# A new table of planner settings for a fused attention and MLP-mixer kernel

## Chip, cores, metric

The kernel runs on one core of a Trainium2 chip. The metric is the device time of one launch in microseconds (us); the figure of a kernel is the median of several runs.

## What is computed

Two blocks read the same input x (2048 tokens of 512) and are mixed by a gate per token: 32-head attention with a head size of 16, and a token-shifting MLP of four weight matrices with two layer norms and two GELUs. Everything is bf16 in memory.

```python
def _A_ref(x, wqkv, wo):
    qkv = (x @ wqkv).reshape(B, S, 3, H, Dh)      # S=2048, H=32, Dh=16
    scores = jnp.einsum("bhqd,bhkd->bhqk", q, k) * (Dh ** -0.5)
    p = softmax(scores, axis=-1)
    o = jnp.einsum("bhqk,bhkd->bhqd", p, v)
    return o.reshape(B, S, D) @ wo

def _B_ref(x, w1, w2, w3, w4):
    h = gelu(layernorm(x) @ w1)
    # the four quarters of h's channels are shifted by 1, -1, 2 and -2 tokens
    hs = shifted(h) @ w2
    x1 = x + hs
    return x1 + gelu(layernorm(x1) @ w3) @ w4     # w3: 512 x 1792

g = sigmoid((x * gate_w).sum(-1, keepdims=True))
out = g * _A_ref(x, ...) + (1 - g) * _B_ref(x, ...)
```

## The kernel before

**Tiles.** A score tile is 128 keys by 512 queries of one head: 32 heads, 16 key blocks and 4 query blocks make 2048 of them. A *round* is a query block, a group of eight heads and one of its two halves, so four heads and 64 tiles; there are 32 rounds. TensorE makes a score tile with one matmul on 32 of its rows (L1320) into one of eight PSUM banks. The exponential is then taken in one of two ways.

- *On ScalarE (ACT):* `issue_act` takes two tiles in two banks and one ACTIVATE turns both into bf16 probabilities (L1415, 128x1024). One matmul per tile then multiplies them into the round's accumulator bank (L1544). The planner costs it with `hold = 0.833 * 512 * w + 51.5` ns for w tiles.
- *On VectorE (DVE):* `issue_dve` takes one tile, and one TENSOR_SCALAR writes 16-bit integers whose bits, read as bf16, are an approximate power of two (L1446, 128x512; called p1 below). Two such tiles are a *pair*. `close_pair` gives the pair three more copies with a constant added to the bits, each one instruction on 128x1024, here called a *shift*; the four copies are summed by the accumulating matmuls, four per tile where an ACT tile has one. A shift runs on DVE or on GpSimd (POOL); both are at L1489/L1491.

`close_pair` (L1466) decides the engine of the three shifts of each pair. It adds `GP2` to a counter and, when that passes one, the pair is *both*: one shift on DVE, two on POOL. It adds `1 - GP3` to a second counter and, when that passes one, the pair is *alone*: all three on DVE. A pair that starts when no more than `URG` tiles (`URG_L` in the last round) of its round are left is alone too, and alone wins over both. Any other pair has two shifts on DVE and one on POOL.

**The other work.** The projections, the MLP matmuls (L953, L964) and their evacuations on DVE, the GELUs on ACT (L1187, L1224) and the layer norms are woven into the same stream with due positions.

**The order.** Everything is issued in an order that is worked out when the kernel is built: `Sim` is a small event model with a fixed duration for every operation. `run` steps through it; whenever TensorE is free, `pe_pick` (L1718) chooses what goes next, and `try_engine` (L330) takes the job of lowest priority number that is ready for each other engine. The chosen start times sort the emission (L1915), so each engine's instruction stream is fixed. The chip only adds semaphore waits: a matmul waits until the last reader of its bank is done, an ACTIVATE waits for its matmuls, and a POOL operation waits for the last DVE operation placed ahead of it in `in_port_order` (L315), which keeps a single order among the operations that share a port of SBUF.

`pe_pick` is steered by some forty settings in `K`. They start from `BASE` (L505), and every eight score tiles (`SEG = 8`, 256 segments) the entry of `STEPS` (L530) for that segment, where there is one, overwrites some of them. Those the prediction speaks of, besides the three above:

- `LIMD` (L1401): new matmul groups other than ACT's start only while fewer than so many banks are held by something else than ACT's tiles and the accumulators.
- `ACC2` (L1514): how many rounds ahead a second accumulator bank may be opened.
- `CAP3`, `CAP2` (L1731): an ACT group of three (two) tiles is taken if ACT then holds no more than so many banks. `CAP3` is 0 in all of the kernel before, so all its groups have two tiles but one.
- `DVE_STOP` (L1373): no DVE tile is taken from a round with so few tiles left; `AHEAD` (L1371): a tile of the next round may be taken once so few are left in this one.

Of the kernel before, what the change touches and what calls it, by code (L numbers as in the profile page):

```python
# [189 lines left out]
class Sim:  # L190
    SWITCH = {"row": 104.0, "col": 104.0, "full": 96.0}
    ISSUE = 4.0
    EARLY = {"ACT": 100.0, "DVE": 75.0}
# [259 lines left out]
def kernel(  # L453
# [52 lines left out]
        P1_PRIO=0.414,  # L506
        S_PRIO=0.38,
        GP2=0.0,
# [19 lines left out]
    )  # L528
    SEG = 8
    STEPS = {  # L530
        0: dict(GP2=0.8, DVE_STOP=13, DVE_ALONE=-158, SL0=60, PRESS=43, DUE_SH=0),
        1: dict(SL0=130, PRESS=26, MAXU=4, ROT=0),
        2: dict(ROT=3),
        3: dict(GP3=0.9, PRESS=15, ROT=1),
        5: dict(S_PRIO=0.625, GP3=0.967, DVE_STOP_L=12, SL0=60, IDLE_NS=700, DVE_WAIT=4, AHEAD2=16, PRESS=26, MAXU=9,
            ROT=2, DUE_SH=-14, AT_SH=34),
        6: dict(AGE=20000, JOIN=1),
        7: dict(PV_IDLE=0.117, MAXU=5, LIMD=4),
        8: dict(GP2=1),
        9: dict(P1_PRIO=0.743),  # L540
        10: dict(E_PRIO=0.25),
        11: dict(ROT=3),
        12: dict(AHEAD=16),
        13: dict(DVE_WAIT=2),
        14: dict(DVE_WAIT=4, AHEAD=9),
        15: dict(B_LOW=8),
        16: dict(URG_L=18, SL0=0),
        17: dict(DVE_STOP=6, URG=8),
        18: dict(AGE=6000),
        20: dict(S_PRIO=0.178, ROT=0),  # L550
        22: dict(DVE_STOP=4, JOIN=0),
        23: dict(LIMD=3),
        24: dict(GP3=1),
        27: dict(E_PRIO=0.1),
        30: dict(E_PRIO=2),
        32: dict(GP3=0.9, SL1=0, AT_SH=118),
        33: dict(DVE_ALONE=2, BRES=2, PV_FULL=0.97),
        34: dict(S_PRIO=0.214, GP2=0),
        35: dict(S_PRIO=0.178, GP2=1, DVE_ALONE=-158, BRES=0, PV_FULL=0.916),
        36: dict(AT_SH=0),  # L560
        38: dict(B_LOW=3, AT_SH=118),
        39: dict(P1_PRIO=0.414, AHEAD2=13, MAXU=3),
        41: dict(DVE_STOP=6),
        42: dict(P1_PRIO=0.279, DVE_STOP=4),
        44: dict(E_PRIO=0.1),
        45: dict(GP3=0.967),
        46: dict(AGE=20000),
        48: dict(E_PRIO=0.4),
        49: dict(DVE_STOP=6, E_PRIO=0.1, AGE=12000),
        50: dict(MAXG=2),  # L570
        51: dict(E_PRIO=0.4),
        52: dict(E_PRIO=2),
        53: dict(AGE=20000),
        54: dict(B_LOW=0, AT_SH=69),
        55: dict(AT_SH=96),
        56: dict(B_LOW=3, AT_SH=118, AGE=12000),
        59: dict(MAXU=4, AFIRST=2),
        61: dict(P1_PRIO=0.312),
        69: dict(MAXG=1),
        70: dict(AHEAD2=24, ROWM=7),  # L580
        71: dict(DUE_SH=-9, AGE=20000),
        72: dict(URG=11, ROWM=5),
        73: dict(DVE_STOP=8),
        74: dict(GP2=0.8, DVE_STOP=4, URG=8, ROWM=7),
        78: dict(AHEAD=3),
        79: dict(PRESS=18),
        86: dict(SL1=60),
        87: dict(URG=5, SL1=0),
        89: dict(GP3=0.9),
        90: dict(B_LOW=2, PV_FULL=0.97),  # L590
        92: dict(ROT=1),
        93: dict(CAP2=5),
        94: dict(SL0=-75, DVE_WAIT=2, HOLE=2),
        95: dict(B_LOW=8, DVE_WAIT=3, DUE_SH=-6),
        96: dict(PV_FULL=0.86),
        97: dict(GP2=0.5, DVE_STOP=6),
        98: dict(DVE_ALONE=500),
        99: dict(URG=11),
        100: dict(DVE_STOP=4, ROWM=99),
        101: dict(JOIN=1),  # L600
        102: dict(IDLE_NS=537, ROT=2, AFIRST=0, AGE=3000, ROWM=7, JOIN=0),
        104: dict(P1_PRIO=0.279),
        105: dict(DVE_ALONE=2),
        106: dict(DVE_ALONE=-158, AHEAD=9),
        107: dict(URG=5),
        108: dict(DVE_ALONE=500, BRES=4, HOLE=3),
        109: dict(URG=3, DVE_ALONE=138),
        111: dict(URG_L=12, IDLE_NS=864),
        112: dict(GP2=0.315),
        113: dict(DVE_ALONE=362),  # L610
        114: dict(ROT=3),
        115: dict(ROT=2),
        116: dict(DUE_SH=16, AGE=12000),
        117: dict(DUE_SH=-6, AGE=3000),
        118: dict(ROT=1),
        119: dict(GP3=0.967, EARLY=64, AGE=20000),
        120: dict(DVE_ALONE=138),
        121: dict(URG=2, PV_FULL=0.947),
        122: dict(GP2=0.15, BRES=0),
        123: dict(DVE_ALONE=-158),  # L620
        124: dict(DVE_STOP=6, SL0=0, JOIN=1),
        126: dict(IDLE_NS=700, HOLE=7),
        127: dict(P1_PRIO=0.55, PV_FULL=0.86),
        128: dict(GP3=1),
        130: dict(PV_FULL=0.97),
        131: dict(EARLY=99, ROWM=3),
        133: dict(URG=8),
        135: dict(P1_PRIO=0.136, GP3=0.967, DVE_STOP_L=14, PRESS=15),
        136: dict(MAXU=9),
        137: dict(GP2=0),  # L630
        138: dict(DVE_STOP=4),
        139: dict(AT_SH=96, JOIN=0),
        140: dict(DVE_ALONE=-81, PV_IDLE=0.731),
        141: dict(GP3=0.633, AHEAD=5, PV_FULL=0.813),
        143: dict(URG=5, MAXU=7),
        145: dict(MAXU=4, ROT=2),
        146: dict(PV_IDLE=0.117),
        147: dict(PV_IDLE=0.731, MAXU=7, ROT=1),
        148: dict(GP2=0.5),
        151: dict(MAXG=2, AGE=12000),  # L640
        152: dict(MAXG=1, AGE=20000),
        153: dict(DUE_SH=-14),
        154: dict(URG=8, AHEAD2=16, HOLE=3),
        155: dict(URG=5, AHEAD2=24, DUE_SH=-6, HOLE=7, MAXG=2, AGE=12000),
        156: dict(S_PRIO=0.38, IDLE_NS=459),
        157: dict(S_PRIO=0.178, DVE_ALONE=138, IDLE_NS=700, DUE_SH=-14, MAXG=1, AGE=3000),
        159: dict(DVE_WAIT=2),
        160: dict(HOLE=3),
        161: dict(DVE_STOP=6),
        162: dict(E_PRIO=0.25),  # L650
        163: dict(AHEAD=12, CAP2=6, LIMA=4),
        167: dict(B_LOW=3, PRESS=26),
        171: dict(S_PRIO=0.3, GP2=1, GP3=0.967, DVE_STOP=13, DVE_STOP_L=16, URG=3, DVE_ALONE=-158, SL0=60, SL1=60,
            IDLE_NS=864, B_LOW=5, DVE_WAIT=3, AHEAD=24, PV_IDLE=0.117, PRESS=18, MAXU=4, AT_SH=69, HOLE=2, MAXG=2,
            E_PRIO=2, AFIRST=2, AGE=6000, ROWM=7, LIMA=3),
        172: dict(DVE_STOP=6),
        173: dict(B_LOW=2),
        174: dict(E_PRIO=0.25),
        175: dict(MAXU=7, HOLE=7),
        176: dict(MAXG=1),  # L660
        177: dict(AT_SH=34),
        178: dict(AT_SH=0),
        179: dict(AT_SH=34),
        180: dict(B_LOW=3, ROWM=5),
        181: dict(ROT=0, GATE=3, ACC2=1),
        184: dict(URG=11),
        185: dict(SL0=0),
        186: dict(S_PRIO=0.178),
        187: dict(IDLE_NS=459),
        188: dict(PV_IDLE=0.5),  # L670
        189: dict(DVE_ALONE=-81),
        190: dict(JOIN=1),
        191: dict(ACC2=0),
        192: dict(S_PRIO=0.214, PV_FULL=0.86, ROWM=3, ACC2=1),
        193: dict(AHEAD=7, PV_FULL=0.947),
        194: dict(PV_FULL=0.97, ROWM=5),
        195: dict(URG=8),
        196: dict(AT_SH=118),
        198: dict(ROT=2),
        199: dict(HOLE=0),  # L680
        200: dict(ROWM=7),
        201: dict(B_LOW=8, AFIRST=0, JOIN=0),
        202: dict(MAXU=3),
        203: dict(MAXU=7),
        204: dict(P1_PRIO=0.743, S_PRIO=0.3, GP2=0, GP3=1, DVE_STOP=4, DVE_STOP_L=7, URG=2, DVE_ALONE=2, EARLY=64,
            SL0=60, SL1=0, IDLE_NS=537, B_LOW=5, DVE_WAIT=2, AHEAD=24, PV_FULL=0.813, PV_IDLE=0.117, MAXU=4, ROT=3,
            DUE_SH=-9, HOLE=7, MAXG=2, CAP2=5, AGE=3000, LIMA=4, JOIN=1),
        205: dict(SL1=60),
        206: dict(DVE_STOP_L=12, SL1=0, MAXU=2, ROT=2, DUE_SH=-14, LIMD=4, ACC2=0, JOIN=0),
        207: dict(SL1=60, AGE=12000),  # L690
        208: dict(SL1=130),
        209: dict(URG=3, ROT=3, ROWM=5),
        210: dict(URG=2, ROT=2, ROWM=7),
        211: dict(DVE_WAIT=4, PV_FULL=0.916, ROT=1, AT_SH=96),
        213: dict(S_PRIO=0.38, HOLE=3),
        214: dict(S_PRIO=0.3, DVE_STOP_L=7, SL0=130, SL1=0, DVE_WAIT=2, PV_FULL=0.813, ROT=2, AT_SH=118, HOLE=7, LIMD=3,
            AGE=3000, JOIN=1),
        215: dict(GP2=0.15),
        216: dict(SL1=-75, PV_IDLE=0.731),
        217: dict(URG=8, B_LOW=8, MAXG=1),  # L700
        220: dict(DVE_STOP=6),
        222: dict(HOLE=3, AGE=20000),
        225: dict(HOLE=7, AGE=3000),
        226: dict(DVE_WAIT=3),
        227: dict(GP2=0.655, CAP2=6),
        228: dict(HOLE=3, GATE=2),
        229: dict(JOIN=0),
        230: dict(GP2=0.15, AT_SH=34, HOLE=7, CAP2=5, GATE=3, ROWM=3, JOIN=1),
        231: dict(B_LOW=3),
        233: dict(PRESS=8),  # L710
        234: dict(GP3=0.9),
        237: dict(DVE_ALONE=138),
        238: dict(PRESS=11),
        239: dict(SL0=-75, MAXU=9, CAP2=4),
        240: dict(URG_L=18, PRESS=18, CAP2=6),
        242: dict(DVE_STOP=13, URG=11, HOLE=2),
        243: dict(MAXU=3),
        246: dict(DVE_STOP=6, URG=8, MAXU=9, HOLE=7),
        248: dict(S_PRIO=0.625, GP2=0.5, PV_FULL=0.86),
        251: dict(PRESS=57),  # L720
        252: dict(SL0=0, LIMA=2),
    }
    K = SimpleNamespace(**BASE)

# [1249 lines left out]
```

## Time and profile before

| what | value |
|---|---|
| median of 3 runs | 754.83 us (753.9 to 755.6) |
| profiled execution, its own time | 750.92 us |
| its span, first to last instruction | 749.1 us |
| ACT busy | 733.0 us (98%), 771 instructions |
| DVE busy | 689.9 us (92%), 1450 instructions |
| POOL busy | 423.3 us (57%), 422 instructions |
| PE busy | 735.9 us (98%), 9516 matmuls |
| DMA | 46 GB/s mean, 17.40 MB read, 6.81 MB written |

Each figure is the union of an engine's instruction spans. Matmul ends are modelled, so PE's 98% doesn't say that TensorE has no room. ACT's and DVE's spans of successive instructions overlap by some 0.1 to 0.2 us, so the pace of a series is read from their start times, not from the mean duration.

The span is cut below into eight stretches of 256 score tiles each, by the start of every 256th matmul of L1320 (at 8.44, 104.17, 199.5, 289.4, 384.94, 470.69, 557.0 and 654.14 us). "DVE busy" is of the stretch; p1 and shifts are counts of instructions that start in it.

| eighth | p1 | shifts on DVE | shifts on POOL | DVE busy us of us |
|---|---|---|---|---|
| 0 | 48 | 24 | 41 | 87.11 of 95.73 |
| 1 | 73 | 51 | 61 | 90.08 of 95.33 |
| 2 | 60 | 45 | 44 | 87.67 of 89.90 |
| 3 | 82 | 74 | 50 | 91.10 of 95.54 |
| 4 | 70 | 77 | 27 | 81.27 of 85.75 |
| 5 | 68 | 50 | 51 | 78.07 of 86.31 |
| 6 | 78 | 70 | 50 | 88.89 of 97.14 |
| 7 | 70 | 74 | 36 | 83.45 of 94.96 |

### The profile page before, as it was taken

To read this page: it belongs to the slowest core of one execution; us is meant where nothing else is said; L and a number is where in the kernel's file an instruction comes from. 1 tells how busy PE (TensorE), PEld (TensorE's weight loads), DVE (VectorE), ACT (ScalarE), POOL (GpSimd) and SP (SyncE) were. 2 spreads that over 40 slices of the span, in tenths; PEclk is the share of its full clock that TensorE was granted. 3 is DMA by queue.
4 is the path that set the end of the run, shared out by engine and by line. 5 is a ranking of instruction groups with operands and counts; after the bars stand their busy time and mean duration, and the time that the engine had idled before them with its cause. 6 is when DMAs were issued, how large, how long until landed. Compare 5 with 4: busy or idle time off the path is not lost.

```text
span 749.1 us, 23684 instructions
## 1 busy us (share of the span) xinstructions
PE 735.9 (98%) x9516; PEld 211.6 (28%) x9516; DVE 689.9 (92%) x1450; ACT 733.0 (98%) x771; POOL 423.3 (57%) x422
## 2 busy tenths in 40 slices
PE   8999999999999999999999999999999999999997
PEld 5343222232222222222322222222222232222222
DVE  5899999998999999999899999998999889989987
ACT  7999999999999999999999999999999999999996
POOL 2355667687674665566555432646767645553552
PEclk9999999999999999999999999999999999999999
DMA  9413322012122211034000110011100000101001
GB/s 197 146 34 85 83 62 49 19 47 79 54 65 68 63 28 49 20 81 109 10 25 9 38 36 27 14 28 47 25 20 21 21 12 28 27 25 21 7 21 47
DMA packets 67095, 34.60 MB, mean 46 GB/s; under 512 B 46749, under 2 KB 62381, under 8 KB 66985
## 3 DMA queue, kind: packets, MB, share of 16 engines
q1 hardware_dynamic: 66040, 32.56, 17.4%
q8 instruction: 74, 1.21, 0.7%
q10 hardware_dynamic: 944, 0.52, 0.2%
q14 instruction: 37, 0.29, 0.1%
HBM read 17.40 MB, written 6.81 MB: 32 GB/s over the span
## 4 chain that ended last, share of the span: by engine, by line
PE 86%; ACT 7%; DVE 4%; issue 2%; POOL 0%; DMA 0%; ACTq 0%; DVEq 0%; POOLq 0%
PE banks L1544 30%; PE banks L1320 30%; PE banks L953 25%; ACT prob L1415 6%; DVE prob L1446 1%; DVE prob L1489 1%; PE banks L932 0%; POOL prob L1491 0%; ACT L1415 0%; DVE st L1128 0%; DVE kT L1025 0%; DMA xn_dram<-xn 0%; PE banks L984 0%; DVE hT L1185 0%; DVE xn L1148 0%
## 5 line engine op out<-in xcount | busy, mean ns | idle before, releaser
L1415 ACT ACTIVATE prob<-banks 128x1024 bf16<-128x1024 f32 x750 | 688.7, 1149 | 1.1 <-PE banks L1320 0.6
L1491 POOL TENSOR_SCALAR prob<-prob 128x1024 uint16<-128x1024 uint16 x360 | 370.2, 1045 | 280.5 <-DVE prob L1489 145.5
L1446 DVE TENSOR_SCALAR prob<-banks 128x512 uint16<-128x512 f32 x549 | 364.1, 684 | 30.3 <-PE banks L1320 25.0
L1544 PE MATMUL banks<-prob,V 128*17 128x512 bf16 (+1 forms) x3695 | 321.3, 382 | 1.2 <-POOL prob L1491 0.7
L1320 PE MATMUL banks<-q,kT 32*128 32x512 bf16 x2048 | 282.7, 385 | 6.1 <-ACT prob L1415 3.4
L1489 DVE TENSOR_SCALAR prob<-prob 128x1024 uint16<-128x1024 uint16 (+1 forms) x465 | 181.2, 434 | 5.3 <-PE banks L1544 2.5
L1320 PEld LDWEIGHTS <-kT 32*128 32x128 bf16 x2048 | 71.1, 91 | 316.4 <-ACT prob L1415 291.0
L1544 PEld LDWEIGHTS <-V 128*17 128x17 bf16 (+1 forms) x3695 | 72.0, 88 | 117.3 <-issue 97.8
L953 PE MATMUL banks<-xnT,w 128*32 128x512 bf16 x1152 | 98.0, 383 | 0.0
L953 PE MATMUL banks<-w,hT 128*32 128x512 bf16 x688 | 63.8, 384 | 0.0
L1583 POOL TENSOR_TENSOR oT<-accsb,bcs 128x512 bf16<-128x512 f32 x31 | 39.8, 1282 | 28.5 <-DVE prob L1489 14.4
L953 PEld LDWEIGHTS <-w 128*32 128x32 bf16 x1936 | 42.4, 95 | 47.3 <-issue 27.7
L953 PE MATMUL banks<-w,w 128*32 128x256 bf16 (+1 forms) x784 | 39.1, 308 | 0.1
L953 PE MATMUL banks<-w,hB 128*32 128x512 bf16 x448 | 37.3, 382 | 0.0
L964 PE MATMUL banks<-wo,oD 32*128 32x512 bf16 x76 | 28.8, 385 | 0.0
L1565 DVE COPY accsb<-banks 128x512 f32<-128x512 f32 x31 | 21.2, 685 | 1.4 <-PE banks L1544 1.0
L1128 DVE BATCH_NORM_STATS2 st<-x_sb 128x6 f32<-128x512 bf16 x32 | 21.8, 685 | 0.0
L953 PE MATMUL banks<-w,wq 128*32 128x512 bf16 x256 | 20.9, 383 | 0.0
L953 PEld LDWEIGHTS <-hT 128*32 128x32 bf16 x688 | 14.8, 95 | 19.1 <-issue 14.9
L953 PE MATMUL banks<-wo,oD 128*32 128x512 bf16 x164 | 20.0, 385 | 0.1
L1217 DVE CAST hB<-banks 128x512 bf16<-128x512 f32 x28 | 19.0, 680 | 1.1 <-PE banks L953 1.1
L1217 DVE CAST hT<-banks 128x512 bf16<-128x512 f32 x28 | 19.0, 680 | 0.4 <-PE banks L953 0.4
(95 smaller groups left out, 262.1 us busy)
## 6 DMA issues: line engine op xcount, KB each, us to landing
bcs<-rr SPq DMA_DIRECT2D x124, 64.0 KB, 2.1
xn_dram<-xn SPq DMA_DIRECT2D x32, 128.0 KB, 1.8
w<-in_B_w_dram SPq DMA_DIRECT2D x5, 512.0 KB, 7.8
oD<-oT SPq DMA_DIRECT2D x124, 16.0 KB, 2.1
w<-in_B_w_dram SPq DMA_DIRECT2D x4, 448.0 KB, 3.2
out_dram<-ot SPq DMA_DIRECT2D x14, 128.0 KB
x_sb<-in_A_x_dram SPq DMA_DIRECT2D x3, 512.0 KB
w<-in_A_wqkv_dram SPq DMA_DIRECT2D x2, 256.0 KB, 5.8
```

The source lines that it names most:

```text
L953: units.append([Op("col", j, lambda j=j, lf=lf, rf=rf, n0=n0, n1=n1, st=st, sp=sp: nc.tensor.matmul(get()[32 * j:32 * j + 32, n0:n1], lhsT ...
L964: o = Op("row", i, lambda: nc.tensor.matmul(get(), lhsT=lf(0, P)[rows], rhs=rf()[rows], start=False, stop=True, tile_position=(32 * i, 0), ...
L1128: a = dve(600, deps, lambda: nc.vector.bn_stats(out=sb.slot[:], in_=x_sb[:, t, :]), prio=6, at=at, acq=[sb])
L1217: pre.append(evac(g, PSUM_NS, lambda ps, m=m: nc.vector.tensor_copy(out=h2()[:, m, :], in_=ps[:])))
L1320: o = Op("row", i, lambda: nc.tensor.matmul(dst(), lhsT=kT[G][32 * i:32 * i + 32, kt * P:(kt + 1) * P], rhs=qbuf[G, c].slot[32 * i:32 * i ...
L1415: job = act(hold, ops, lambda: nc.scalar.activation(out=prob[:, pb.cut(), :].bitcast(BF16), in_=unit()[:, rb.cut(), :], func=ACT.Exp, scal ...
L1446: return nc.vector.tensor_scalar(out=prob[:, b0.cut() if w == 2 else b0.bufs[h0].slot, :], in0=unit()[:, rb.cut() if w == 2 else rb.bufs[0 ...
L1489: return nc.vector.tensor_scalar(out=cut(k), in0=cut(0), scalar1=float(SHIFT * k), scalar2=None, op0=ALU.add)
L1491: return nc.gpsimd.tensor_scalar(out=cut(k), in0=cut(0 if both else 2), scalar1=1.0, scalar2=float(SHIFT * (k if both else 1)), op0=ALU.mu ...
L1544: return nc.tensor.matmul(one(accs[r])[32 * i:32 * i + n, :], lhsT=lhs(n), rhs=rhs(), start=st and not edge, stop=True, tile_position=(0, ...
L1565: e = dve(PSUM_NS, round_ops[r], lambda: nc.vector.tensor_copy(out=ab.slot[:], in_=one(accs[r])), acq=[ab], prio=0, frees=[accs[r], Call(a ...
L1583: n = gp(1250, d3, lambda: nc.gpsimd.tensor_tensor(out=ob.slot[:], in0=ab.slot[:], in1=bb.slot[:], op=ALU.mult), acq=[ob], frees=[ab, bb], ...
```

## The change

The dictionary `STEPS` is replaced as a whole: 185 segments had an entry, 215 have one after. `BASE`, `Sim`, its durations and every function stay as they are, so the same tiles and the same matrices are worked on; what differs is the order of each engine's stream, which score tiles go to DVE instead of ACT, and which engine makes which shift. Nothing is added or removed by hand. The entries for segments 128 to 159, and those elsewhere that set `LIMD` or `CAP3`:

```diff
     STEPS = {
...
-        7: dict(PV_IDLE=0.117, MAXU=5, LIMD=4),
...
-        23: dict(LIMD=3),
...
-        128: dict(GP3=1),
-        130: dict(PV_FULL=0.97),
-        131: dict(EARLY=99, ROWM=3),
-        133: dict(URG=8),
-        135: dict(P1_PRIO=0.136, GP3=0.967, DVE_STOP_L=14, PRESS=15),
-        136: dict(MAXU=9),
-        137: dict(GP2=0),
-        138: dict(DVE_STOP=4),
-        139: dict(AT_SH=96, JOIN=0),
-        140: dict(DVE_ALONE=-81, PV_IDLE=0.731),
-        141: dict(GP3=0.633, AHEAD=5, PV_FULL=0.813),
-        143: dict(URG=5, MAXU=7),
-        145: dict(MAXU=4, ROT=2),
-        146: dict(PV_IDLE=0.117),
-        147: dict(PV_IDLE=0.731, MAXU=7, ROT=1),
-        148: dict(GP2=0.5),
-        151: dict(MAXG=2, AGE=12000),
-        152: dict(MAXG=1, AGE=20000),
-        153: dict(DUE_SH=-14),
-        154: dict(URG=8, AHEAD2=16, HOLE=3),
-        155: dict(URG=5, AHEAD2=24, DUE_SH=-6, HOLE=7, MAXG=2, AGE=12000),
-        156: dict(S_PRIO=0.38, IDLE_NS=459),
-        157: dict(S_PRIO=0.178, DVE_ALONE=138, IDLE_NS=700, DUE_SH=-14, MAXG=1, AGE=3000),
-        159: dict(DVE_WAIT=2),
...
+        61: dict(DVE_STOP_L=7, LIMD=4),
...
+        77: dict(LIMD=4, LIMA=2),
...
+        123: dict(DVE_STOP=6, ROT=2, CAP3=6),
+        124: dict(DVE_STOP=4, ROT=1, CAP3=0),
...
+        129: dict(DVE_STOP=8, IDLE_NS=374, E_PRIO=0.25),
+        130: dict(DVE_STOP=4, IDLE_NS=864, E_PRIO=2),
+        131: dict(GP2=0.655, GP3=1, SL1=0, B_LOW=2, PV_FULL=0.97, PRESS=18, MAXU=4, E_PRIO=0.4),
+        132: dict(DVE_STOP=8, CAP3=6),
+        134: dict(ROT=3),
+        136: dict(ROT=0),
+        137: dict(CAP3=0),
+        138: dict(SL0=-75),
+        140: dict(P1_PRIO=0.312, ROT=3, DUE_SH=32),
+        142: dict(P1_PRIO=0.279, ROT=0, DUE_SH=-6),
+        144: dict(GP3=0.9, MAXU=3),
+        145: dict(CAP2=6),
+        146: dict(URG=11),
+        147: dict(S_PRIO=0.38),
+        148: dict(GP3=0.8),
+        149: dict(GP3=0.9),
+        150: dict(GP3=0.8),
+        151: dict(GP2=0.8),
+        152: dict(DVE_STOP=4),
+        153: dict(GP3=0.9, PV_IDLE=0.5),
+        155: dict(GP2=0),
+        156: dict(GP2=0.8),
+        157: dict(GP2=0),
+        158: dict(GP2=0.8, GP3=0.8),
...
+        251: dict(CAP3=6),
```

The settings that decide the shifts, averaged over the 32 segments of each eighth of the table (before / after):

| eighth | GP2 | GP3 | URG | LIMD |
|---|---|---|---|---|
| 0 | 0.95 / 0.82 | 0.97 / 0.93 | 6.4 / 4.9 | 3.50 / 3.00 |
| 1 | 0.97 / 0.95 | 0.94 / 0.93 | 8.0 / 4.4 | 3.00 / 3.09 |
| 2 | 0.86 / 0.92 | 0.95 / 0.98 | 7.3 / 3.8 | 3.00 / 3.91 |
| 3 | 0.39 / 0.22 | 0.92 / 0.95 | 5.1 / 5.8 | 3.00 / 3.19 |
| 4 | 0.23 / 0.60 | 0.78 / 0.93 | 5.6 / 5.9 | 3.00 / 3.00 |
| 5 | 0.83 / 0.90 | 0.85 / 0.91 | 5.7 / 9.0 | 3.00 / 3.03 |
| 6 | 0.42 / 0.58 | 0.99 / 0.96 | 5.9 / 2.9 | 3.25 / 3.38 |
| 7 | 0.28 / 0.36 | 0.93 / 0.99 | 8.4 / 7.6 | 3.00 / 3.88 |

Over the whole table `DVE_STOP` is 5.7 before and 7.2 after on average, `AHEAD` 12.4 and 9.8, and `ACC2` is 1 in 24 and 58 of the 256 segments. `LIMD` is 4 in 24 segments before (7 to 22, 206 to 213) and 80 after (61 to 73, 77 to 101, 107, 179, 212 to 251). `CAP3` is 6 in eight segments after (123, 132 to 136, 249, 251).

## The prediction

> **What bounds the kernel now.** I read the page's table of groups first, then the waits, then two pieces of the timeline, then the list of one line's durations.
>
> ```profile
> L1415 ACT ACTIVATE prob<-banks 128x1024 bf16<-128x1024 f32 x750 | 688.7, 1149 | 1.1 <-PE banks L1320 0.6
> L1491 POOL TENSOR_SCALAR prob<-prob 128x1024 uint16<-128x1024 uint16 x360 | 370.2, 1045 | 280.5 <-DVE prob L1489 145.5
> L1446 DVE TENSOR_SCALAR prob<-banks 128x512 uint16<-128x512 f32 x549 | 364.1, 684 | 30.3 <-PE banks L1320 25.0
> ...
> L1489 DVE TENSOR_SCALAR prob<-prob 128x1024 uint16<-128x1024 uint16 (+1 forms) x465 | 181.2, 434 | 5.3 <-PE banks L1544 2.5
> ```
>
> The exponentials keep ACT busy for 688.7 us and it sat idle ahead of them for 1.1 us in all. With the GELUs and table loads ACT has 733.0 of 749.1 us. From the first exponential at 8.87 us to the end of the last at 740.76 us nothing but ACT's own work sets the pace; ahead and behind lie a start and a tail of about 8 us each that the diff doesn't touch.
>
> ```profile
> PEld L1320 <- ACT prob L1415: 291.0, 657, 1.6
> ...
> DVE prob L1446 <- PE banks L1320: 25.0, 66, 1.3
> ```
>
> Columns: who waited for whom, us in total, times, longest. TensorE's weight loads for a score tile wait 657 times for ACT to give a bank back, though the chain of waits names PE for 86% of the span: PE follows ACT, it doesn't hold it up. The second row is DVE's largest wait: p1 stands still until its score tile is made.
>
> ```profile
> 399.35 13.03 ACT L1415 ACTIVATE prob<-banks 128x1024 bf16<-128x1024 f32 x14
> ```
> ```profile
> 404.39 0.42 DVE L1489 TENSOR_SCALAR prob<-prob 128x1024 uint16<-128x1024 uint16 x1
> 404.72 0.69 DVE L1446 TENSOR_SCALAR prob<-banks 128x512 uint16<-128x512 f32 x1
> 405.32 0.42 DVE L1489 TENSOR_SCALAR prob<-prob 128x1024 uint16<-128x1024 uint16 x1
> 405.65 0.69 DVE L1446 TENSOR_SCALAR prob<-banks 128x512 uint16<-128x512 f32 x1
> ```
>
> Columns: start, length, instruction. Fourteen exponentials in 13.03 us, the last of 1.15: (13.03 - 1.15)/13 = 0.914 us of pace; 688.7/750 gives 0.918, which I use. On DVE a p1 is followed after 0.60 us and a shift after 0.33 us, though their spans are 0.69 and 0.42.
>
> So the time can fall by one thing above all: fewer ACT pairs. Two score tiles that go to DVE take one ACTIVATE away, 0.918 us, or 0.459 us a tile. What limits the DVE tiles is DVE itself, busy 689.9 of 749.1 us.
>
> **The change, part by part.** No operation is new in kind except the ACT groups of three; the counts and places move.
>
> *Shifts from DVE to POOL.* By the rule of `close_pair` a share a = (1 - GP3) + GP3 x URG/64 of the pairs is alone and GP2 x (1 - a) both, so a pair has 2 + a - GP2 x (1 - a) shifts on DVE. I tried this on the kernel before: with the table's averages by eighth it gives 1.30, 1.38, 1.43, 1.83, 2.13, 1.58, 1.73 and 1.96 a pair; weighted with the p1 counts of the trace (half of 48, 73, 60, 82, 70, 68, 78, 70) that makes 464 shifts on DVE, where the trace has 465. The new table gives 1.44, 1.32, 1.23, 1.94, 1.65, 1.52, 1.56 and 1.82: 433 at the same number of tiles. So 30 shifts leave DVE, most of them in eighth 4 (0.48 x 35 = 17), which was 95% busy. At 0.33 us that frees 10 us of DVE. One more DVE tile costs there 0.60 + 0.33 x 1.58/2 = 0.86 us, and shortens DVE's span by the 0.459 us that ACT no longer needs, so the freed time carries 10/(0.86 + 0.46) = 7.6 tiles and the end moves by 7.6 x 0.459 = **-3.5 us**. What hides the other side: POOL takes the 30 shifts at 1.01 us of pace, from successive starts (its spans of 1.045 overlap a little), 30 us more beside 423.3 busy, with 280.5 us of idle time ahead of its shifts. TensorE gets six more matmuls for a pair (eight instead of two), 7.6/2 x 6 = 23 of 0.38 us, four at a time, 2 us spread over waits of 291 us. Without POOL's cover the shifts would have to go back, and the 3.5 us with them. Bounds: 0, if the freed time stays idle, and 5.3 us, if the rule is off by half as much again.
>
> *Blocked shifts.* A shift on DVE has a median of 421 ns, a mean of 434 and a maximum of 1380:
>
> ```profile
> L1489 DVE TENSOR_SCALAR prob<-prob x465: 293/421/1380, 12.0 to 739.7; 128x1024 uint16<-128x1024 uint16 x154, 128x512 uint16<-128x512 uint16 x1
> ```
>
> The excess, 465 x 13 ns = 6 us, lies in a few that run about as long as a POOL operation; over 391 large POOL operations that is 15 ns each, and 30 more make 0.5 us of DVE, 0.2 us of the end: **+0.2**. The Trainium skill ("SBUF — State Buffer", section "SBUF: two separate sides") says that a VectorE operation in a two-port mode and a GpSimd operation exclude one another for a whole instruction. By it, the 30 could each hold up DVE in full; this is the last rival below.
>
> *Groups of three.* `CAP3` is 6 in eight segments, 64 tiles, about 47 of them ACT's: at most 15 groups. No row has a 128x1536 ACTIVATE. It costs at most one and a half pairs, 1.377 us; per element the GELU row (6178 ns for 7168, 0.862 ns) would give 1.32. The gain is 0 to 15 x 0.055 = 0.8 us; a score row is nearer than a GELU row, so **-0.3**.
>
> *More banks for DVE.* `LIMD` = 4 allows a fourth bank outside ACT's, now in 80 segments. DVE waited 25.0 us for score tiles; in the last four eighths it has 32 us of idle time in 364. Where `LIMD` was 4 before (31 to 80 us) DVE is 46.56 of 48.60 busy, while from 628 to 726 us, where it becomes 4, it is 90.44 of 98.03. If that stretch reached the same 96% it would gain 3.5 us of DVE, 2.6 tiles, 1.2 us; the higher `DVE_STOP` and lower `AHEAD` (fewer tiles on offer at a round's end) pull the other way. Bounds -2.5 (both stretches of it) and +2.5; I take **-0.6**.
>
> The remaining settings (priorities, the order among rows, when MLP work starts) change places without an added or removed instruction. Their sum shows in ACT's waits: 1.1 us ahead of exponentials, and 2.8 us ahead of three table loads after the GELUs. These can at best vanish, -3.9 us, and have no cheap upper end (second rival); I take 0.
>
> Sum: -3.5 + 0.2 - 0.3 - 0.6 = **-4.2 us**. The profiled execution took 750.92 us (span 749.1, 1.8 around it), so a like one takes 746.7. The median of the runs shown is 3.9 us above the profiled one; carried over, the forecast is 754.8 - 4.2 = **750.6 us**. In counts: 3.5 + 0.6 = 4.1 us at 0.459 us are some 9 more DVE tiles, so 4 to 5 ACT pairs fewer, and up to 15 groups of three in place of 22 pairs.
>
> **Rivals.**
>
> *The later eighths fill up too.* DVE idles 32 us of 364 in eighths 4 to 7, but 2.2 of 89.9 in eighth 2. At 5% idle it would have 14 us more there: 11 tiles, 5.0 us, together -9.2: **745.6**. For it: nothing of ACT or POOL stands in the way. Against it: MLP evacuations are spread differently there, and DVE's waits for score tiles come from banks that ACT holds.
>
> *ACT is starved of banks (slower).* The fourth bank outside ACT's, and `ACC2` = 1 in 58 segments, come out of the same eight banks. Place: the exponentials of the 80 segments, 640 tiles, about 234 pairs. Price: where an exponential came late before, it was by 0.03 to 0.28 us, 0.11 in the mean (15 times, from successive ends). Once 38 pairs are late by that, the 4.2 us are gone; with one in three late it is 78 x 0.11 = 8.6 us: **759.2**. For it: 291 us of waits of score tiles for ACT's banks show that banks are the tight thing. Against it: with `LIMD` 4 from 31 to 80 us ACT was 48.16 of 48.60 us busy.
>
> *Nothing gained.* The tiles on offer, not DVE's time, set the count; freed time stays idle: **754.8**. Against it: DVE is 95% busy and more from 104 to 471 us.
>
> *POOL shuts DVE out.* Each of the 30 POOL operations costs DVE its 1.01 us; half of these 30 us vanish in its 59 us of idle time, ACT waits for the rest: 750.6 + 15 = **766**. Against it: 391 such operations cost 6 us so far. The Trainium skill's rule has the trace on its side in that stretched shifts exist, but not for this price: they make 15 ns a POOL operation.
>
> **How the numbers follow.** Forecast 0.45, fuller eighths 0.18, starved ACT 0.20, nothing gained 0.14, POOL 0.03. The likeliest gives 750.6. A range of 743 to 760 leaves out a part of the fuller case, the far end of the starved one and the last, together about 0.2; the forecast's own is 747 to 754, from its bounds. A measurement tells 0.2%, 1.5 us, from no change. Faster: 0.45 + 0.18 + a little of the third rival = 0.65. Same: 0.13. Slower: 0.22.
>
> **What would show it.** Right: some 737 to 747 ACTIVATEs on scores, 555 to 565 p1, shifts on DVE near 430 to 445 and on POOL near 390 to 400, fewest lost in eighth 4; ACT's idle time ahead of L1415 still under 3 us. DVE's share of idle time as before means that the shifts alone did it; a fall in eighths 5 to 7 means the first rival. More than 5 us of waits ahead of exponentials in the `LIMD` stretches means starvation. Stretched shifts beyond 12 us of excess means POOL. The forecast is wrong in its root if p1 stays at 549 or falls.

## The result and the profile after

The changed kernel takes **746.93 us** (median of 6 runs, 746.08 to 747.91) against 753.86 us for the kernel before (6 runs beside it and earlier, 751.18 to 755.60). The ratio is 0.9914, with a 95% interval of 0.9899 to 0.9929: 6.5 us faster, within 1.1 of that. The profiled execution took 746.63 us, with a span of 744.8 us (first to last instruction), 4.3 us shorter than the span of before.

The costliest groups of the changed kernel, from the same table of its page (the code has moved down by 46 lines: L1461 was L1415, L1492 was L1446, L1535 and L1537 were L1489 and L1491):

```profile
L1461 ACT ACTIVATE prob<-banks 128x1024 bf16<-128x1024 f32 x747 | 686.1, 1144 | 0.9 <-PE banks L1590 0.3
L1537 POOL TENSOR_SCALAR prob<-prob 128x1024 uint16<-128x1024 uint16 x402 | 413.5, 1046 | 240.5 <-DVE prob L1535 102.6
L1492 DVE TENSOR_SCALAR prob<-banks 128x512 uint16<-128x512 f32 x552 | 365.6, 684 | 31.1 <-PE banks L1366 24.9
...
L1535 DVE TENSOR_SCALAR prob<-prob 128x1024 uint16<-128x1024 uint16 x429 | 166.9, 434 | 7.9 <-PE banks L1590 3.5
```

There are three exponentials fewer, 36 shifts fewer on DVE and 42 more on POOL. Kept apart by shape, the same groups show what the counts hide:

```profile
L1461 ACT ACTIVATE prob<-banks 128x1024 bf16<-128x1024 f32 x745 | 684.4, 1144 | 0.9 <-PE banks L1590 0.3 <-PE banks L1366 0.2
...
L1492 DVE TENSOR_SCALAR prob<-banks 128x1024 uint16<-128x1024 f32 x2 | 2.4, 1219 | 0.0
...
L1461 ACT ACTIVATE prob<-banks 128x1536 bf16<-128x1536 f32 x1 | 1.5, 1458 | 0.0
```

So 745 pairs, one group of three and one single tile on ACT (1494 tiles, before 1499), and 550 single and two double p1 on DVE (554 tiles, before 549). Five score tiles went to DVE, and of fifteen possible groups of three one came about.

The second difference is on ACT just behind the first GELU. The timeline of ACT, before and then after:

```profile
162.12 7.04 ACT L1187 ACTIVATE hT<-hT 128x8192 bf16<-128x8192 bf16 x1
170.54 1.28 ACT L1415 ACT_TABLE_LOAD   x1 [1.38 <-PE banks L1544]
171.83 4.69 ACT L1415 ACTIVATE prob<-banks 128x1024 bf16<-128x1024 f32 x5
```
```profile
168.53 7.03 ACT L1233 ACTIVATE hT<-hT 128x8192 bf16<-128x8192 bf16 x1
175.57 1.28 ACT L1461 ACT_TABLE_LOAD   x1
176.87 3.98 ACT L1461 ACTIVATE prob<-banks 128x1024 bf16<-128x1024 f32 x4
```

The load of the exponential's table stands behind a wait that the first exponential had for TensorE: 1.38 us before, nothing after. The profile puts it down to products (L1544); no score tile was made between 168.42 us and the load. At the other two returns from a GELU the waits were 0.83 and 0.56 us and are 0.85 and 0.02.

The account of the 4.3 us between the two profiles, with one pair at 0.917 us and the group of three at 1.343 (both the distance of successive ends in the trace). An exponential is called *late* by the time that its end lies more than 0.917 us behind the end of the one ahead of it:

| term | us |
|---|---|
| four pairs fewer, one group of three more: -4 x 0.917 + 1.343 | -2.3 |
| waits ahead of the three table loads (and 0.04 us of one other), 2.81 to 0.85 | -2.0 |
| late exponentials elsewhere, 1.65 to 1.41 | -0.2 |
| a small exponential of the gate's, set in without a gap | -0.5 |
| first exponential 0.17 later, tail 0.51 longer | +0.7 |
| sum | -4.3 |

The medians, though, are 6.9 us apart (6.5 by the ratio). The remaining 2.6 us (2.2) aren't in these two profiles; the first experiment looks for them.

### The profile page after: what moved, and what is told of

Same layout as the page of the kernel before. It is cut to its first block, busy times and chain, and to the rows that moved or that the text cites. A ratio compares the mean times of both kernels' runs of the same rounds, so it can differ in the third digit from the quotient of the medians.

```text
span 744.8 us, 23763 instructions
## 1 busy us (share of the span) xinstructions
PE 732.9 (98%) x9539; PEld 215.9 (29%) x9539; DVE 682.8 (92%) x1417; ACT 730.2 (98%) x768; POOL 466.5 (63%) x464
## 4 chain that ended last, share of the span: by engine, by line
PE 78%; ACT 12%; DVE 3%; issue 3%; POOL 2%; DMA 1%; SPq 0%; DVEq 0%; POOLq 0%; ACTq 0%
PE banks L1590 28%; PE banks L1366 27%; PE banks L999 22%; ACT prob L1461 11%; POOL prob L1537 1%; DVE prob L1535 1%; DVE prob L1492 1%; PE banks L978 0%; POOL oT L1629 0%; DMA pk<-den 0%; DMA bcs<-rr 0%; PE banks L1923 0%; SPq L1633 0%; PE banks L1030 0%; ACT L1461 0%
## 5 line engine op out<-in xcount | busy, mean ns | idle before, releaser
L1461 ACT ACTIVATE prob<-banks 128x1024 bf16<-128x1024 f32 x747 | 686.1, 1144 | 0.9 <-PE banks L1590 0.3
L1537 POOL TENSOR_SCALAR prob<-prob 128x1024 uint16<-128x1024 uint16 x402 | 413.5, 1046 | 240.5 <-DVE prob L1535 102.6
L1492 DVE TENSOR_SCALAR prob<-banks 128x512 uint16<-128x512 f32 x552 | 365.6, 684 | 31.1 <-PE banks L1366 24.9
L1590 PE MATMUL banks<-prob,V 128*17 128x512 bf16 (+1 forms) x3710 | 315.8, 381 | 0.6 <-POOL prob L1537 0.5
L1366 PE MATMUL banks<-q,kT 32*128 32x512 bf16 x2048 | 279.1, 384 | 4.8 <-ACT prob L1461 2.0
L1535 DVE TENSOR_SCALAR prob<-prob 128x1024 uint16<-128x1024 uint16 x429 | 166.9, 434 | 7.9 <-PE banks L1590 3.5
L999 PE MATMUL banks<-xnT,w 128*32 128x512 bf16 x1152 | 88.8, 383 | 0.1
L999 PE MATMUL banks<-w,hT 128*32 128x512 bf16 x688 | 59.5, 383 | 0.0
L1010 PE MATMUL banks<-wo,oD 32*128 32x512 bf16 x64 | 23.8, 384 | 0.0
```

Of the source, the lines that this page charges most:

```text
L999: units.append([Op("col", j, lambda j=j, lf=lf, rf=rf, n0=n0, n1=n1, st=st, sp=sp: nc.tensor.matmul(get()[32 * j:32 * j + 32, n0:n1], lhsT ...
L1010: o = Op("row", i, lambda: nc.tensor.matmul(get(), lhsT=lf(0, P)[rows], rhs=rf()[rows], start=False, stop=True, tile_position=(32 * i, 0), ...
L1366: o = Op("row", i, lambda: nc.tensor.matmul(dst(), lhsT=kT[G][32 * i:32 * i + 32, kt * P:(kt + 1) * P], rhs=qbuf[G, c].slot[32 * i:32 * i ...
L1461: job = act(hold, ops, lambda: nc.scalar.activation(out=prob[:, pb.cut(), :].bitcast(BF16), in_=unit()[:, rb.cut(), :], func=ACT.Exp, scal ...
L1492: return nc.vector.tensor_scalar(out=prob[:, b0.cut() if w == 2 else b0.bufs[h0].slot, :], in0=unit()[:, rb.cut() if w == 2 else rb.bufs[0 ...
L1535: return nc.vector.tensor_scalar(out=cut(k), in0=cut(0), scalar1=float(SHIFT * k), scalar2=None, op0=ALU.add)
```

## The experiments

They ran in three groups of four, each beside the kernel before, whose medians there were 753.23, 754.24 and 752.21 us; the ratios are to those. Distances to the changed kernel use its 746.93 us, though it didn't run beside them as it is; where one is about 1 us, the interval of the ratio decides.

### The kernel before, profiled again

No edit.

> The kernel before, unchanged, profiled once more. The medians differ by 6.9 us between the two kernels, the two profiled spans only by 4.3 (749.1 and 744.8). Theory A (the profiled execution of before was one of its quick ones): the median stays 753 to 755 and this profile, if it falls on a slower execution, has a span of 751 to 754 with its extra 2 to 5 us in ACT waits at one or two places. Theory B (a profiled execution is always shorter than the rest): span 749 again and no new waits.

Median 754.54 us (12 runs, 752.82 to 758.67), ratio 1.0014 (0.9991 to 1.0037). The profiled execution took 757.22 us, its span was 755.4: theory A, with 1.4 us more than it allowed. Neither profile is of a typical execution. The first one's 750.92 us is less than any of the 75 runs of this kernel beside the experiments took (751.07 to 758.89), and of the 12 runs here only one took longer than the second one's 757.22. Windows of 5 us, first of the first profile of before, then of this one (length; busy time and count of PE, PEld, DVE, ACT, POOL; granted clock; DMA share; GB/s):

```profile
70.00:75.00 5.00, 4.97 (x67) 1.27 (x59) 4.51 (x13) 5.00 (x7) 1.20 (x2) 1.00 0.29 91
75.00:80.00 5.00, 5.00 (x61) 1.35 (x59) 4.54 (x9) 4.84 (x6) 4.46 (x5) 1.00 0.53 106
80.00:85.00 5.00, 5.00 (x73) 1.69 (x73) 4.20 (x11) 5.00 (x7) 2.87 (x3) 1.00 0.36 93
```
```profile
70.00:75.00 5.00, 2.91 (x34) 0.63 (x26) 3.64 (x11) 2.84 (x4) 2.05 (x3) 0.84 0.23 64
75.00:80.00 5.00, 5.00 (x38) 0.81 (x34) 3.63 (x10) 3.47 (x4) 0.45 (x1) 0.50 0.50 111
80.00:85.00 5.00, 5.00 (x48) 1.03 (x45) 2.04 (x4) 3.42 (x4) 4.54 (x5) 0.64 0.38 63
```

In 15 us ACT does 9.73 us of work instead of 14.84; over the whole execution its late exponentials add up to 7.95 us instead of 1.65, and these 6.3 us are the difference of the two spans. The chain of waits of this execution shows how it begins and what it becomes (start, length, what):

```profile
68.32 3.02 DMA pk<-den
...
71.36 0.25 DVE pk L1572
...
72.69 1.03 ACT prob L1415
...
73.72 0.61 PE banks L1320 x2
74.33 0.96 PE banks L1544 x7
75.30 0.54 PE banks L1320 x3
...
84.29 0.33 PE banks L1320 x4
84.61 0.54 PE banks L1544 x8
```

The reciprocal of the second round's denominators (L1572) stands in DVE's stream before its transfer has landed. DVE waits 2.91 us (0.13 in the first profile; why the transfer lands later here isn't shown), TensorE runs out of probabilities, and its granted clock halves. For ten microseconds a step of score tiles takes 0.54 us instead of 0.33 and one of eight products 0.96 instead of 0.54, too slow for ACT's 0.917 us. The runs with a halved clock are the long ones, but they don't make the median: of the 75 runs, the 14 with a mean granted clock under 0.996 have a median of 757.0 us, the 52 with 0.998 or more still one of 752.9, 2 us above the first profile.

The changed kernel has no such stretch in the same 15 us (ACT busy 15.00); the transfer that it meets too early, 1.29 us in the third round at 92.8 us, cost ACT 0.06 us.

### Table loads that don't wait

In both kernels, behind the GELU of the first MLP and the second of each later pair:

```diff
+            nc.scalar.activation(out=mb[:].bitcast(F32), in_=zero[:, 0:1], func=ACT.Exp)
```

> Kernel before, with a one-element exponential put behind each of the three last GELU instructions, so that the table load for the exponentials runs while TensorE still makes the next score tiles. Order and tile choice are unchanged. Theory (ACT's own work and its few waits are the time): the waits of 1.38, 0.83 and 0.56 us ahead of the table loads now overlap the loads of 1.28 us; 1.28 + 0.83 + 0.56 = 2.7 us less, minus 3 x 0.2 us for the small instruction: -2.1 us, near 752. Rival (what ACT waits for there, the DVE and PE work ahead of the first score tiles, moves the end anyway): no change, within 0.5 us.

> The same three small instructions in the changed kernel, whose waits ahead of the table loads are 0.02, 0.85 and 0.02 us. Theory: 0.85 us less minus 0.6 us for the instructions: -0.3 us, near 746.7, so that the distance between the two kernels shrinks from 6.9 to about 5 us. Rival: the distance stays at 6.9 us.

The kernel before went to 750.89 us, ratio 0.9961 (0.9942 to 0.9979): -2.9 us by the ratio, with an interval of -1.6 to -4.4, and -2.3 by the medians, where -2.1 was expected. The changed one stayed: 747.02 us. Its gap of 0.85 us is gone too, but its profile has 2.4 us of late exponentials instead of 1.4. The load now runs at once (timeline of ACT, kernel before with the edit):

```profile
165.34 7.04 ACT L1188 ACTIVATE hT<-hT 128x8192 bf16<-128x8192 bf16 x1
172.40 1.28 ACT L1189 ACT_TABLE_LOAD   x1
173.69 0.20 ACT L1189 ACTIVATE mb<-zero 128x1 f32<-128x1 bf16 x1
173.80 2.83 ACT L1424 ACTIVATE prob<-banks 128x1024 bf16<-128x1024 f32 x3
```

With it the two kernels are 3.9 us apart. So in the old order closing these gaps gains about what they promise, and the changed order's shorter gaps are a real part of the gain. Two later pairs of runs, with and without the early loads, say the same: 2.4 and 1.8 us.

### What an ACT instruction costs

Every 37th score exponential of the changed kernel is issued twice:

```diff
+        def ex(twice=evs["x"] % 37 == 18):
+            for _ in range(1 + twice):
+                inst = nc.scalar.activation(...)
...
```

> Changed kernel with 20 of its 747 score exponentials done twice, evenly spread. Theory (ACT is the bound at every place): 20 x 0.917 = +18.3 us, near 765. Rival (TensorE or DVE bounds in part, ACT only looks full because its spans overlap): less than +12 us.

767.97 us, ratio to before 1.0185 (1.0152 to 1.0218): +21.0 us for 20, or 1.05 us each: theory, with a little more than the pace. In the trace the surplus lies in the repeat itself: it writes the same buffer, starts 0.03 us after its original has ended instead of overlapping it, and so ends 1.056 us behind it, 0.139 beyond the pace. So ACT's added work came out in full, 20 x 1.056 = 21.1 us: ACT is the bound, as the prediction had it. The run adds work; that taking away four pairs gains the same per instruction (2.3 us) is inferred from it.

### What DVE work costs in a fixed order

Two edits of the changed kernel that leave the planner's order and tile choice as they are. In the first, one shift of every fifth pair of the kind with two POOL shifts goes back to DVE; in the second, every 27th p1 is issued twice.

```diff
-                if alone or k == 1 or k == 2 and not both:
+                if (alone or k == 1 or k == 2 and not both) != moved:
...
```

> Changed kernel, order and tile choice kept, but in every fifth of the 157 pairs with two shifts on POOL the first of these runs on DVE at the same place: 32 shifts go back to DVE, 32 x 0.335 = 10.7 us of DVE work (and 32 us less on POOL), which undoes the shift part of the change alone. Theory (DVE's time is what allows this tile choice): DVE falls behind and the time rises by 3 to 11 us, to 750 to 758. Rival (DVE has 62 us of idle time and hides it, the engine of a shift is nearly free once the order stands): within 1.5 us of 746.9.

```diff
+        def p1(twice=evs["y"] % 27 == 13):
+            for _ in range(1 + twice):
+                inst = nc.vector.tensor_scalar(...)
...
```

> Changed kernel with 20 of its 552 score operations on DVE (p1) done twice, evenly spread: 20 x 0.60 = 12 us more of DVE, beside the 20 doubled exponentials that cost 21 us. Theory (DVE's price in a fixed order is a part of ACT's): +3 to +8 us. Rival A (DVE binds everywhere): +12 us or more. Rival B (its 62 us of idle time hide it): under +1.5 us.

The 32 shifts cost 1.0 us by the medians (747.93 us, ratio 0.9927, interval 0.9902 to 0.9951, which holds the changed kernel's 0.9914, so it may be nothing): the rival. DVE did them, as its group shows, with its idle time falling from 62.0 to 56.6 us:

```profile
L1539 DVE TENSOR_SCALAR prob<-prob 128x1024 uint16<-128x1024 uint16 x461 | 180.8, 436 | 6.3 <-PE banks L1596 3.1 <-ACT prob L1461 0.7 <-POOL prob L1541 0.6
```

Twenty doubled p1, about as much DVE work (12 us), cost 5.7 us (752.66 us, 0.9982, 0.9967 to 0.9998), as the theory had it. The cost shows on ACT: in this profile its late exponentials add up to 6.1 us instead of 1.4, and one table load waits 1.85 us instead of 0.85. The two edits differ in what they hold: a p1 keeps its PSUM bank until it ends, a shift holds none and takes work off POOL. That this is why one costs and the other doesn't is argued, not shown.

### Trying to mend the old order at 70 us

Two edits of the kernel before, four runs. In the first, the reciprocal, product and onward transfers of the second round come 2.5 us later in the order, with and without the early loads; in the second, the whole chain up to POOL's product and its transfers, 3.5 us later, again with and without.

```diff
-        self.emit(self.t, ...)
+        self.emit(self.t + getattr(j.fn, "later", 0.0), ...)
...
+        if r in (1,):
+            for x in [r1, r2, d2] + d3:             # second edit: also n and d4
+                x.fn.later = 2500.0                 # second edit: 3500.0
```

> Kernel before; only in the second round (r = 1) the reciprocal of the denominators, the product with the gate and the five transfers behind them are emitted 2.5 us later in the order. In two profiles of this kernel DVE stood still there for 2.91 and 3.25 us on the transfer of the denominators, TensorE ran dry, its granted clock fell to 0.5 to 0.84 for some ten microseconds and ACT lost 4 to 6 us; in the first profile the wait was 0.13 us. Theory (this one exposed transfer makes most of the 2.6 us by which the medians differ more than the first two spans): median 2 to 3 us lower, near 751, and the runs closer together than the 7 us of before. Rival (the spread of the runs has another cause, or the wait only moves to the next operation): no change within 0.7 us, same spread.

> Kernel before with the later reciprocal of the second round and with the early table loads. Theory: the two repairs are independent, so about 2.9 + 2.5 us are gained, near 748.2; what is then left to the changed kernel (746.9) is 1 to 2.5 us, the price of the 5 score tiles that it gives to DVE (5 x 0.459 = 2.3 us). Rival (the gain is mostly in the tile choice): 750 or more.

> Kernel before; in the second round the whole chain from the reciprocal on (reciprocal, product, transfers, POOL's normalising product and the four transfers of its result) is emitted 3.5 us later, so that POOL, too, meets it later. With the reciprocal alone moved, POOL stood still on its product instead and the median was 756.4. Theory (this chain of transfers is the one place where the old order has no room): neither DVE nor POOL waits for it, the ACT loss at 70 to 92 us falls under 1.5 us, the median to about 751 and the runs lie within 3 us. Rival (the region is short of DVE and POOL time whatever the chain does): 753.5 or more.

> Kernel before with the whole chain of the second round 3.5 us later and the early table loads. Theory: 751 - 2.5 = 748.5; the changed kernel's 746.9 then stands 1 to 2.5 us lower for its 5 score tiles (2.3 us). Rival: 751 or more, as the region has no room.

The theory missed in all four. In the last three the rival's bound held, 750, 753.5 and 751 us or more; the first came out worse than both. The later reciprocal gave 756.36 us (ratio 1.0028, 1.0009 to 1.0047), with the early loads 753.94 us (0.9995, 0.9981 to 1.0009). The later chain gave 754.13 us (1.0009, 0.9989 to 1.0030), with the loads 752.33 us (0.9987, 0.9971 to 1.0004). In the first, DVE no longer waits for the denominators (it waits 1.5 us for another transfer, L1148's), but POOL, whose product is next in its own stream, stands still for 3.5 us, and behind it its shifts; the chain of waits of that execution:

```profile
82.04 0.17 POOL oT L1586
...
83.27 2.07 POOL prob L1491 x2
...
85.38 0.39 PE banks L1544 x3
85.77 0.32 PE banks L1320 x3
86.09 0.94 PE banks L1544 x8
```

Two POOL shifts come late, the products of L1544 wait for them, and the step of eight products again takes 0.94 us. With the whole chain moved, POOL still waited 4.0 us for `bcs<-rr`. The late exponentials between 70 and 95 us, summed for each profile of this order: 0.7 us in the first, then 6.2 (again), 4.3 (early loads), 5.9 and 6.6 (later reciprocal), 2.7 and 4.6 (later chain). Elsewhere they add up to 1.0 to 1.7 us in each of the seven. So the loss is in that stretch whenever it is there, and the first profile was the exception; which of its transfers would have to come earlier isn't settled, and no edit here took it away. It also needs no halved clock, against what the first of these four expectations says of two profiles: with the early loads ACT lost 4.3 us there at a granted clock of 1.00.

### The same in the changed kernel

Early loads, and the chain of the third round 2.5 us later.

> Changed kernel with both repairs, the chain moved in its third round (by 2.5 us), where its DVE waits 1.29 us for the denominators. Theory: at most the 0.4 us of late exponentials at 97 us and 0.2 us net from the table load: 746.3, a gain of 0.3 to 0.8 us. Rival: no change, or a loss of up to 2 us as in the old order when the reciprocal was moved.

747.23 us (ratio 0.9921, 0.9895 to 0.9948): no change. Nothing tried here beats the changed kernel as it is.

### One setting put back

`GP3` of all segments as in the old table, everything else as in the new one.

```diff
-        16: dict(GP3=0.633, URG=2, ACC2=0),
+        16: dict(URG=2, ACC2=0),
...
```

> Changed kernel with one setting of the table, GP3, put back to its old values in all segments (mean 0.944 to 0.916). By the rule of the prediction this is 277 pairs x 0.028 x 1.67 = 13 shifts more on DVE, 4.3 us, or 3 tiles and 1.5 us: 748.4. Theory (every entry is made for the state that the entries ahead of it leave, so a mean says nothing): the planner then gives DVE 539 score tiles instead of 554, which alone is 15 x 0.459 = 6.9 us, with new waits on top: 760 or more. Rival (the means carry the gain): 747 to 750.

786.34 us (2 runs), ratio 1.0439 (1.0393 to 1.0485), worse than either table: theory, and worse than its bound. Who waited for whom, longest first in total, ACT alone:

```profile
ACT prob L1437 <- PE banks L1342: 15.9, 15, 6.7
ACT prob L1437 <- PE banks L1566: 11.0, 8, 3.8
```

The tile count explains 6.9 us of the 39; most of the rest is ACT waiting for score tiles (L1342) and, through TensorE, for products (L1566), one wait being 6.7 us. A mean over the table said how many shifts would go where; it said nothing of what the order would be worth.

## Why the prediction was right, and where it wasn't

**The bound** was read rightly. ACT's pace set the time, and work added to it came out in full. The start and the tail, said to be untouched, together grew by 0.7 us.

**The shifts** came as the rule of `close_pair` said: 429 on DVE for 433, 402 on POOL for 390 to 400, and in eighth 4 the largest fall, from 77 to 55, where the rule gives 58. (The list of signs has "fewest lost in eighth 4"; the sum ahead of it has most of them there, and that was so.) By eighth the rule is off by up to 7, and the errors partly cancel.

**The tiles that they should buy** are the term that was mis-sized: -3.5 us, and -0.6 for the banks, stood for 9 tiles; there were 5, worth 2.3 us, and 552 p1 where 555 to 565 were the sign. The step that failed is "the freed time carries 7.6 tiles". DVE's idle time rose from 59.2 to 62.0 us, so part of the freed time stayed idle, as in the rival that gains nothing. "Without POOL's cover the shifts would have to go back, and the 3.5 us with them" is refuted for the finished order: 32 shifts put back cost 1.0 us, which isn't clear of zero. What holds the number of tiles while the order is made isn't shown.

**Blocked shifts** cost next to nothing, as forecast: 29 that ran longer than 435 ns, with 7.1 us of excess, against 26 with 6.7 before. The rival in which POOL shuts DVE out falls.

**Groups of three** were sized at up to fifteen and -0.3 us; there was one, which saved 1.375 - 1.343 = 0.03 us.

**The remaining settings**, "I take 0" with up to -3.9 us allowed, gave -2.0 us in the gaps ahead of the table loads. The size failed: the prediction names the 2.8 us of these gaps and counts none of them as gained. Which entries closed them isn't shown.

**Carrying the 3.9 us** between profile and median over to the changed kernel failed. Its median is 0.3 us above its profiled execution. The old order has a stall of its own at 70 to 92 us, 2.7 to 6.6 us in six of its seven profiles, which the first one hardly had. The account of the profiles of before and after leaves 2.6 us of the 6.9 to it; that the stall is all of them is inferred from its size and from the profiles, which differ little elsewhere, since no edit removed it alone.

The forecast of -4.2 us was thus met in direction and within the wide range partly by luck, as errors of opposite sign partly cancelled: too much for the tiles, nothing for the gaps and the stall. 746.93 us lies just below the forecast's own range of 747 to 754, and nearer to the 745.6 of the fuller eighths, whose mechanism didn't come. Of the rivals, starved ACT didn't come (0.9 us of idle time ahead of exponentials, with `LIMD` 4 in 80 segments), and DVE didn't fill the later eighths: in eighths 4 to 7 its idle time rose from 32.5 to 38.4 us (in eighth 4 it is busy 74.56 of 85.86 us, where it was 81.27 of 85.75).

## What to carry to other kernels

When one engine is at its pace from end to end, count its instructions and then list every gap it has, also the few of a microsecond: gaps ahead of table loads can be worth as much as instructions, and one profile may miss the ones that come and go between executions. Before one profile is subtracted from another, compare each with the median of its own kernel. And a table of settings that was searched step by step is one object: an average over it can predict how often something happens, but putting one column back cost 39 us where the whole change was worth 7.

## What the hardware showed that wasn't expected

A short stall of TensorE can cost far more than itself. In the second profile of before its matmuls stood still for 1.38 and 0.68 us between 71 and 74 us; the granted clock was then 0.50 from 75 to 80 us and 0.64 in the next five. Four of seven profiles of the old order have a stretch of half clock between 73 and 92 us, one of six of the new order with its own tile choice has one, at 55 us.

The Trainium skill ("TensorE: Matmul & The Clock Gate", section "Part 1: The HAM clock gate (the "warmup" mystery)") says that the clock halves after an idle window of about 3.4 us. Here the clock halved at 73.40 us, and in the 3.41 us ahead of that TensorE was idle for only 1.8 us, in pieces. Nor does the idle time alone decide it. The first line is this stretch, the second one from the profile with the later chain (length, busy time of PE next, granted clock third from the end):

```profile
69.99:73.40 3.41, 1.64 (x23) 0.40 (x15) 2.04 (x8) 1.92 (x3) 1.05 (x2) 1.00 0.11 24
84.29:87.70 3.41, 1.65 (x26) 0.66 (x29) 1.96 (x5) 1.35 (x2) 1.71 (x2) 1.00 0.13 39
```

Matmuls cover the same time in both; the next 3.41 us had a granted clock of 0.50 in the first case and of 1.00 in the second. And ahead of the half clock of the new order at 55 us, in the run with 32 shifts put back, matmuls cover 3.38 of 3.41 us. What sets the halving off isn't shown.
